# Halves of a batch in turn, joint PE stretches and one written order in a fused attention and two-layer kernel on one core

## The chip, the cores and the metric

The kernel runs on one core of a Trainium2 chip. The metric is the device time in microseconds of one execution; for the kernel before, three runs gave 732.37, 733.7 and 735.04 us, median 733.7 us.

## The reference

For 8 batches of 8 heads, 576 tokens, 64 channels per head and 32 memory slots per head, attention goes through slots. Then a two-layer network runs on all 4608 tokens.

```python
a = softmax(phi, axis=2)                    # per head, over the 576 tokens
k_m, v_m = a^T k, a^T v                     # 32 slots x 64 channels
attn = softmax(q k_m^T / 8, axis=-1)        # over the 32 slots
x = heads of (attn v_m) side by side        # 4608 x 512
h = x @ w_in                                # 512 x 2048
g = where(h > 0, h, exp(min(h, 0)) - 1)     # ELU
out = g @ w_out                             # 2048 x 512
```

## The kernel before

The product of v_m with w_in is taken first (the "w_in product", step `vw`), so that the 2048 hidden channels of a batch come straight from the probabilities: hidden = probabilities times (v_m w_in). All large products run as three passes over a high and a low part of each operand.

**Work items.** A batch has 16 blocks of 128 hidden channels (j) and two halves of 288 tokens (hf). One item is one (batch, half, block); items count from 0 to 255, 32 per batch. An item goes through these steps: `hidden` on PE (L657, six matmuls of 288 columns into one of two PSUM banks named psh), `elu_exp` on ACT (L672, L673), `elu_max` on DVE (L684 for the first 256 tokens, L686 for the other 32, which go to the tile `rest`), `elu_high` on ACT (L698), `elu_low` on DVE (L704), and `project` on PE (L712, six matmuls of 512 columns, into two accumulator banks of the half: pso00 and pso01 for half 0, pso10 and pso11 for half 1). After the last block `collect` copies the accumulators out (ACT and DVE) and `store` writes them. The 32 left-over tokens of each half are gathered for a pair of batches and projected at the pair's end, in eight steps `rest_high`, `rest_low`, `rest_project` that use pso00, then `rest_store`.

**The attention of a batch** is made during the batch before: `load_phi`, `load_e`, `load_kv`, `load_q` on SP's queue; `phi_max` on DVE (L407); `spread_max`, which writes the maxima to DRAM (nmd, L276) and reads them back into all partitions (nmb, L278); `e_shift` on POOL (L289) and `e_exp` on ACT (L294); `slots` (80 small matmuls, L453) and `slots_transpose` (L487) on PE; `scores` for three units of 192 tokens (`by_head`, L502, 64x32 tiles of the array); per unit a softmax on DVE and ACT: `turn`, `softmax_max`, `softmax_shift`, `softmax_exp`, `softmax_sum`, `softmax_divide`, `turn_back`, `probs_high`, `probs_low`. The w_in product is made in four chunks of 512 hidden channels (also `by_head`, L502), each copied out by `vw_high` on ACT (L605) and `vw_low` on DVE (L611). Scores and w_in products share two PSUM banks named psb.

**What sets the order.** Batches 0 and 1, and the attention of batch 2, follow a written list (FIRST) on all engines. After it, each step has a place, a number on the scale of items, and steps are issued in order of places: `hidden` of item i at i - 1.7, `elu_high` at i - 1, `project` at i + 0.6. From there on only PE and SP keep that order; ACT, DVE and POOL take theirs from the framework's scheduler. In batches 2 to 7 the items go block by block with the two halves alternating, so all four accumulators are in use throughout.

```python
    with tc.manual_schedule(engines={mybir.EngineType.PE, mybir.EngineType.SP}):
        with tc.manual_schedule():
            for f, a in first:
                f(*a)
        for _, _, f, a in plan:
            f(*a)
```

Of the kernel before, what the change touches and what calls it, by code (L numbers as in the profile page):

```python
# [16 lines left out]
P = 128  # L17
# [158 lines left out]
def fused_kernel(ctx: ExitStack, tc: tile.TileContext, phiT, phi, kv0, kvt, kv, q0, q1, w_in, w_out, out):  # L176
# [67 lines left out]
    def bank(shape, where):  # L244

        pool, name = {
            "b": (ps_b, "psb"), "h": (ps_h, "psh"),
            "x": (ps_o, "pso01"), "y": (ps_o, "pso10"), "z": (ps_o, "pso11"),
        }[where]
        return pool.tile(shape, F32, name=name)  # L250
# [73 lines left out]

    def load_half_q(b, hf):
        t = work.tile([P, NPAIR, HALF], F32, name="qh", tag="osb", bufs=2 * NB)
# [191 lines left out]

    def turn(b, u):
# [80 lines left out]
    def vw_high(b, c, n0=0, n1=CW):  # L600
        s = st[b]
        if s["vw"][c] is None:
            s["vw"][c] = work.tile([P, 2, 2, CW], F32R, name="vw", tag="vw", bufs=NVB)
        for a, ps in enumerate(s["ps"]["vw", c, n0]):
            nc.scalar.copy(s["vw"][c][:, HI, a, n0:n1], ps)  # L605

    def vw_low(b, c, n0=0, n1=CW):
        s = st[b]
        t = s["vw"][c]
        for a, ps in enumerate(s["ps"].pop(("vw", c, n0))):  # L610
            nc.vector.tensor_tensor(  # L611
                t[:, LO, a, n0:n1], ps, t[:, HI, a, n0:n1], ALU.subtract
            )

# [6 lines left out]
    for b, j0, j1 in blocks:  # L628
# [4 lines left out]
        ]:  # L633
# [42 lines left out]
    def elu_max(it):  # L676
# [7 lines left out]
        nc.vector.scalar_tensor_tensor(gf[:, :n], gf[:, :n], -1.0, ps[:, :n], ALU.add, ALU.max)  # L684
        o = (b % 2 * 2 + hf) * REST
# [43 lines left out]
    def collect(it, t):  # L729
        b, hf, j = order[it]  # L730
        if (b, hf) not in osbs:
            osbs[b, hf] = work.tile([P, NT, DM], F32, name="osb", tag="osb", bufs=2 * NB)
# [52 lines left out]
    def warm_up(n):  # L785
# [8 lines left out]
        for f in (  # L794
# [5 lines left out]
            elu_exp, elu_max, rest_copy, elu_high, elu_low, project, collect, store, rest_high, rest_low,  # L800
# [18 lines left out]
    def softmax(b, u, o, step):  # L819
        at(o, turn, b, u)  # L820
        at(o + step, softmax_max, b, u)
        at(o + 1.01 * step, softmax_shift, b, u)
        at(o + 2 * step, softmax_exp, b, u)
        at(o + 3 * step, softmax_sum, b, u)
        at(o + 3.01 * step, softmax_divide, b, u)
        at(o + 4 * step, turn_back, b, u)
        at(o + 5 * step, probs_high, b, u)
        at(o + 6 * step, probs_low, b, u)

    def products(b, c, o, *cols):  # L830
        at(o, vw, b, c, *cols)
        at(o + (0.3 if cols else 0.75), vw_high, b, c, *cols)
        at(o + (0.31 if cols else 0.76), vw_low, b, c, *cols)

    def attention(b, o):
        at(o - 4, load_phi, b)
# [98 lines left out]
```

## Time and profile before

| what | value |
|---|---|
| median of three runs | 733.7 us (732.37 to 735.04) |
| span of the profiled execution | 730.5 us |
| PE matmul, busy | 706.8 us (97%) |
| PE weight load, busy | 571.2 us (78%) |
| DVE, ACT, POOL, busy | 467.1, 464.9, 44.6 us |
| granted TensorE clock, mean | 0.995 |
| DMA | 64.46 MB, mean 88 GB/s |

The page gives the span, from the first to the last instruction; the profiled execution's own device time is not given apart from it, and the median of the runs lies 3.2 us above the span. A busy share near 100% on PE with the others near 65% says which engine to follow; what share of that busy time is switching or refilling is seen only in the timeline, by the distance from one start to the next.

### The profile page before, as it was taken

What the parts mean: (1) busy time and instruction counts of PE and PEld (TensorE: products, weight loads), DVE (VectorE), ACT (ScalarE), POOL (GpSimd) and SP (SyncE); (2) the same over time, 40 slices, a digit from 0 to 9 for tenths busy, and PEclk for the clock granted to TensorE, in tenths of its full rate; (3) what the DMA queues carried; (4) which work ended last, traced back from release to release, by engine and by line L of the source; (5) the groups of instructions that cost most, each with busy time, mean ns of one, the idle gap of its engine ahead of it and who ended that gap; (6) DMA issues with size and microseconds to landing.
All of it is one profiled execution on the core that took longest, in us unless ns stands there. A gap on an engine that the chain in (4) does not pass through costs nothing.

```text
span 730.5 us, 13669 instructions
## 1 busy us (share of the span) xinstructions
PE 706.8 (97%) x5114; PEld 571.2 (78%) x5114; DVE 467.1 (64%) x1253; ACT 464.9 (64%) x1110; POOL 44.6 (6%) x88
## 2 busy tenths in 40 slices
PE   6698999999999999999999999999999999999997
PEld 5566887887768878877788777887787887888886
DVE  4999898886495467544954449545774547754442
ACT  4779988886456656755655656656565565666552
POOL 0011111122000100010000100000000010000000
PEclk9899999999999999999999999999999999999999
DMA  8961404432316010611015110260002600010002
GB/s 308 369 240 57 175 30 120 146 101 62 102 64 208 27 43 1 247 36 45 2 57 183 56 45 1 76 206 28 19 1 72 223 28 18 1 58 0 2 1 73
DMA packets 24978, 64.46 MB, mean 88 GB/s; under 512 B 3408, under 2 KB 7632, under 8 KB 24912
## 3 DMA queue, kind: packets, MB, share of 16 engines
q1 hardware_dynamic: 24816, 63.46, 25.9%
q8 instruction: 41, 0.67, 0.4%
q14 instruction: 25, 0.20, 0.1%
q10 hardware_dynamic: 96, 0.13, 0.1%
HBM read 54.13 MB, written 9.44 MB: 87 GB/s over the span
## 4 chain that ended last, share of the span: by engine, by line
PE 72%; DMA 12%; DVE 8%; issue 3%; ACT 3%; POOL 1%; SPq 1%; POOLq 0%; DVEq 0%; ACTq 0%
PE pso L712 43%; PE psh L657 22%; DMA nmd<-nm 5%; PE psb L502 4%; DMA nmb<-nmd 3%; DMA ph<-phiT 3%; PE psb L453 2%; POOL e L289 1%; DMA win<-w_in 1%; DMA e<-phi 1%; DVE top L373 1%; DVE gf L681 1%; ACT gf L673 1%; DVE nm L407 1%; DVE vw L611 1%
## 5 line engine op out<-in xcount | busy, mean ns | idle before, releaser
L712 PE MATMUL pso<-wout,gp 128*128 128x512 f32 x1728 | 448.3, 397 | 3.0 <-DVE gp L704 2.3
L712 PEld LDWEIGHTS pso<-wout,gp 128*128 128x128 f32 x1728 | 309.2, 188 | 83.8 <-ACT gf L673 13.0
L657 PEld LDWEIGHTS psh<-A,vw 128*128 128x128 f32 x1536 | 229.2, 188 | 37.5 <-issue 6.2
L657 PE MATMUL psh<-A,vw 128*128 128x288 f32 x1536 | 250.0, 298 | 6.9 <-DVE rest L686 3.4
L684 DVE SCALAR_TENSOR_TENSOR gf<-gf,psh 128x256 f32<-128x256 f32 x192 | 80.5, 419 | 130.1 <-ACT gf L673 129.8
L672 ACT ACTIVATE gf<-psh 128x288 f32<-128x288 f32 x256 | 104.7, 409 | 86.0 <-PE psh L657 84.2
L698 ACT CAST gp<-gf 128x256 fp32r<-128x256 f32 x256 | 103.5, 404 | 87.1 <-DVE gf L684 73.5
L704 DVE TENSOR_TENSOR gp<-gf,gp 128x256 fp32r<-128x256 f32 x256 | 107.6, 421 | 55.2 <-ACT gp L698 54.9
L673 ACT ACTIVATE gf<-gf 128x288 f32<-128x288 f32 x256 | 113.7, 444 | 7.8
L611 DVE TENSOR_TENSOR vw<-psb,vw 128x512 fp32r<-128x512 f32 (+2 forms) x74 | 43.3, 602 | 11.3 <-ACT vw L605 11.1
L289 POOL TENSOR_TENSOR e<-e,nmb 128x512 f32<-128x512 f32 (+1 forms) x18 | 19.7, 1121 | 376.2 <-DMA nmb<-nmd 255.9
L681 DVE SCALAR_TENSOR_TENSOR gf<-gf,psh 128x288 f32<-128x288 f32 x64 | 28.9, 451 | 17.1 <-ACT gf L673 15.9
L605 ACT CAST vw<-psb 128x512 fp32r<-128x512 f32 (+2 forms) x74 | 37.1, 523 | 2.9 <-PE psb L502 0.7
L502 PE MATMUL psb<-win,kvm 64*32 64x512 f32 (+2 forms) x592 | 35.8, 538 | 0.0
L694 POOL COPY rest<-gf 128x32 f32<-128x32 f32 x64 | 24.3, 380 | 165.9 <-DVE gf L681 165.8
L686 DVE SCALAR_TENSOR_TENSOR rest<-gf,psh 128x32 f32<-128x32 f32 x192 | 34.1, 179 | 0.1
L752 ACT CAST gp<-rest 128x256 fp32r<-128x256 f32 x32 | 13.0, 406 | 23.8 <-PE pso L712 21.8
L373 DVE SCALAR_TENSOR_TENSOR top<-mag,top 128x512 uint32<-128x512 uint32 x32 | 22.2, 693 | 1.9 <-ACT mag L364 0.3
L757 DVE TENSOR_TENSOR gp<-rest,gp 128x256 fp32r<-128x256 f32 x32 | 13.4, 418 | 15.0 <-ACT gp L752 14.9
L368 ACT ACTIVATE mag<-raw 128x512 uint32<-128x512 uint32 x30 | 20.1, 672 | 2.5 <-DVE top L373 2.5
L294 ACT ACTIVATE e<-e 128x512 f32<-128x512 f32 (+1 forms) x18 | 9.8, 559 | 16.4 <-POOL e L289 16.3
L364 ACT ACTIVATE mag<-raw 128x512 f32<-128x512 f32 x30 | 19.5, 666 | 0.4 <-DVE win L385 0.4
(96 smaller groups left out, 369.2 us busy)
## 6 DMA issues: line engine op xcount, KB each, us to landing
kvt<-kv SPq DMA_DIRECT2D x32, 512.0 KB, 7.3
out<-osb SPq DMA_DIRECT2D x16, 512.0 KB, 2.8
raw<-w_in SPq DMA_DIRECT2D x15, 512.0 KB, 7.1
raw<-w_out SPq DMA_DIRECT2D x15, 512.0 KB, 8.1
qt<-q SPq DMA_DIRECT2D x18, 384.0 KB, 4.2
ph<-phiT SPq DMA_DIRECT2D x7, 576.0 KB, 4.8
e<-phi SPq DMA_DIRECT2D x12, 256.0 KB, 6.4
qh<-q SPq DMA_DIRECT2D x4, 576.0 KB, 11.5
```

The costliest lines, as they stand in the source:

```text
L502: nc.tensor.matmul(outs[a][32 * j : 32 * j + 32, :], lhs[r, 32 * j : 32 * j + 32], rhs[r, j], start=True, stop=True, tile_position=(64 * a ...
L605: nc.scalar.copy(s["vw"][c][:, HI, a, n0:n1], ps)
L611: nc.vector.tensor_tensor(t[:, LO, a, n0:n1], ps, t[:, HI, a, n0:n1], ALU.subtract)
L657: nc.tensor.matmul(ps, t[:, x, g, c0 : c0 + P], s["A"][hf][:, y, g, :], start=(n == 0), stop=(n == 5),)
L672: nc.scalar.activation(gf, ps, AF.Relu, scale=-1.0)
L673: nc.scalar.activation(gf, gf, AF.Exp, scale=-1.0)
L681: nc.vector.scalar_tensor_tensor(gf, gf, -1.0, ps, ALU.add, ALU.max)
L684: nc.vector.scalar_tensor_tensor(gf[:, :n], gf[:, :n], -1.0, ps[:, :n], ALU.add, ALU.max)
L686: nc.vector.scalar_tensor_tensor(rest_of(b, j)[:, o : o + REST], gf[:, n:], -1.0, ps[:, n:], ALU.add, ALU.max)
L698: nc.scalar.copy(gp[:, HI], gs[it][:, : NT * P])
L704: eng.tensor_tensor(gp[:, LO], gf[:, : NT * P], gp[:, HI], ALU.subtract)
L712: nc.tensor.matmul(ps, gp[:, y], wout[j][:, x, :], start=(first and n == 0), stop=(last and n == 2),)
```

## The change

In batches 2 to 7 the items now go through all 16 blocks of half 0 and then of half 1. The accumulators of the half that is not running are idle, and `scores_of` and `products` borrow them: the three units of scores become one stretch on PE (place base - 14.6, base being the batch's first item), and the four w_in chunks become two stretches of two (base - 7.1 and base + 2.9). Since every chunk is needed by both halves, all four are kept: the fourth takes a buffer ("c3") that holds the queries and the output of batch 1 earlier. `elu_rest` is split from `elu_max`, and is placed later for the first two items of batches 4 and 6, while the rests of the pair before are still read. All steps of the attention have new places, counted from o = base - 32, and after FIRST all engines follow places; FIRST itself is the same text.

```diff
@@ -245,7 +245,8 @@
         pool, name = {
             "b": (ps_b, "psb"), "h": (ps_h, "psh"),
-            "x": (ps_o, "pso01"), "y": (ps_o, "pso10"), "z": (ps_o, "pso11"),
+            "w": (ps_o, "pso00"), "x": (ps_o, "pso01"),
+            "y": (ps_o, "pso10"), "z": (ps_o, "pso11"),
         }[where]
         return pool.tile(shape, F32, name=name)
@@ -322,8 +323,19 @@
         nc.sync.dma_start(t, q1[b - NB, :, u])
         st[b]["q"][u] = t
+    late_c = {}
+    def half_of_1(hf):
+        if "t" not in late_c:
+            late_c["t"] = work.tile([P, 2, NPAIR * HALF], F32, name="one", tag="c3", bufs=1)
+        return late_c["t"][:, hf]
     def load_half_q(b, hf):
-        t = work.tile([P, NPAIR, HALF], F32, name="qh", tag="osb", bufs=2 * NB)
+        if b == 0:
+            t = work.tile([P, NPAIR, HALF], F32, name="qh", tag="osb", bufs=2)
+        else:
+            t = half_of_1(hf).rearrange("p (a n) -> p a n", a=NPAIR)
         t0 = hf * HALF
         nc.sync.dma_start(t, q0[b, :, hf])
         for u, (u0, u1) in enumerate(units(b)):
@@ -516,6 +528,16 @@
         by_head(ps, s["kvm"][:, 0], q)
         s["ps"]["s", u] = ps
+    def scores_of(b, own, lent):
+        s = st[b]
+        first = [bank([P, 2, UT], x) for x in own]
+        last = [bank([P, UT], x) for x in lent]
+        for u in range(NU):
+            ps = [x[:, u] for x in first] if u < 2 else last
+            by_head(ps, s["kvm"][:, 0], s["q"][u])
+            s["ps"]["s", u] = ps
     def turn(b, u):
         s = st[b]
@@ -597,28 +619,21 @@
         by_head(ps, s["kvm"][:, 1], win[c][:, :, n0:n1])
         s["ps"]["vw", c, n0] = ps
-    def vw_high(b, c, n0=0, n1=CW):
+    def vw_high(b, c, n0=0, n1=CW, parts=(0, 1)):
         s = st[b]
         if s["vw"][c] is None:
-            s["vw"][c] = work.tile([P, 2, 2, CW], F32R, name="vw", tag="vw", bufs=NVB)
-        for a, ps in enumerate(s["ps"]["vw", c, n0]):
-            nc.scalar.copy(s["vw"][c][:, HI, a, n0:n1], ps)
-    def vw_low(b, c, n0=0, n1=CW):
+            home = dict(tag="c3", bufs=1) if b >= NB and c == NVC - 1 else dict(tag="vw", bufs=NVB)
+            s["vw"][c] = work.tile([P, 2, 2, CW], F32R, name="vw", **home)
+        for a in parts:
+            nc.scalar.copy(s["vw"][c][:, HI, a, n0:n1], s["ps"]["vw", c, n0][a])
+    def vw_low(b, c, n0=0, n1=CW, parts=(0, 1)):
         s = st[b]
         t = s["vw"][c]
-        for a, ps in enumerate(s["ps"].pop(("vw", c, n0))):
+        for a in parts:
             nc.vector.tensor_tensor(
-                t[:, LO, a, n0:n1], ps, t[:, HI, a, n0:n1], ALU.subtract
+                t[:, LO, a, n0:n1], s["ps"]["vw", c, n0][a], t[:, HI, a, n0:n1], ALU.subtract
             )
     blocks = [(0, 0, 4), (1, 0, 4), (0, 4, 8), (1, 4, 12), (0, 8, 16), (1, 12, 16)]
     blocks += [(b, 0, NJ) for b in range(NB, B)]
@@ -630,7 +645,7 @@
         seen.add(b)
         for hf, j in turns if len(order) == 0 else [
             (hf, j) for j in range(j0, j1) for hf in range(2)
-        ]:
+        ] if b < NB else [(hf, j) for hf in range(2) for j in range(NJ)]:
             order.append((b, hf, j))
             ends.append((new, j == j0, j == j1 - 1))
@@ -682,6 +697,12 @@
             return
         n = NT * P
         nc.vector.scalar_tensor_tensor(gf[:, :n], gf[:, :n], -1.0, ps[:, :n], ALU.add, ALU.max)
+        gs["ps", it] = gf, ps
+    def elu_rest(it):
+        b, hf, j = order[it]
+        gf, ps = gs.pop(("ps", it))
+        n = NT * P
         o = (b % 2 * 2 + hf) * REST
         nc.vector.scalar_tensor_tensor(
             rest_of(b, j)[:, o : o + REST], gf[:, n:], -1.0, ps[:, n:], ALU.add, ALU.max
@@ -729,7 +750,11 @@
     def collect(it, t):
         b, hf, j = order[it]
         if (b, hf) not in osbs:
-            osbs[b, hf] = work.tile([P, NT, DM], F32, name="osb", tag="osb", bufs=2 * NB)
+            if b == 1:
+                o = half_of_1(hf)[:, : NT * DM].rearrange("p (t n) -> p t n", t=NT)
+            else:
+                o = work.tile([P, NT, DM], F32, name="osb", tag="osb", bufs=2)
+            osbs[b, hf] = o
         osb = osbs[b, hf][:, t, :]
         ps = acc[b, hf][t]
         if not ends[it][0]:
...
@@ -816,59 +841,71 @@
         if (f, a) not in done:
             plan.append((place, len(plan), f, a))
-    def softmax(b, u, o, step):
-        at(o, turn, b, u)
-        at(o + step, softmax_max, b, u)
-        at(o + 1.01 * step, softmax_shift, b, u)
-        at(o + 2 * step, softmax_exp, b, u)
-        at(o + 3 * step, softmax_sum, b, u)
-        at(o + 3.01 * step, softmax_divide, b, u)
-        at(o + 4 * step, turn_back, b, u)
-        at(o + 5 * step, probs_high, b, u)
-        at(o + 6 * step, probs_low, b, u)
-    def products(b, c, o, *cols):
-        at(o, vw, b, c, *cols)
-        at(o + (0.3 if cols else 0.75), vw_high, b, c, *cols)
-        at(o + (0.31 if cols else 0.76), vw_low, b, c, *cols)
+    def softmax(b, u, o, *steps):
+        turned, shifted, exped, divided, back, parts = (o + x for x in steps)
+        at(turned, turn, b, u)
+        at(shifted, softmax_max, b, u)
+        at(shifted + 0.01, softmax_shift, b, u)
+        at(exped, softmax_exp, b, u)
+        at(divided, softmax_sum, b, u)
+        at(divided + 0.01, softmax_divide, b, u)
+        at(back, turn_back, b, u)
+        at(parts, probs_high, b, u)
+        at(parts + 0.01, probs_low, b, u)
+    def products(b, o, c, lent, *copies):
+        for i, own in enumerate(("bb", lent)):
+            at(o, vw, b, c + i, 0, CW, own)
+        for n, x in enumerate(copies):
+            at(o + x, vw_high, b, c + n // 2, 0, CW, (n % 2,))
+            at(o + x + 0.01, vw_low, b, c + n // 2, 0, CW, (n % 2,))
     def attention(b, o):
-        at(o - 4, load_phi, b)
+        at(o + 0.5, load_phi, b)
+        for u in range(3):
+            at(o + 1 + 0.1 * u, load_e, b, u)
+        at(o + 3.5, phi_max, b)
+        at(o + 3.6, spread_max, b)
         for c in range(NCH):
-            at(o - 3 + c, load_kv, b, c)
+            at(o + 3.7 + 0.01 * c, load_kv, b, c)
+        at(o + 3.8, load_q, b, 0)
+        for g in range(2):
+            at(o + 5.5 + g, phi_exp, b, g)
+        at(o + 7.5, slot_scale, b)
         for u in range(3):
-            at(o + 4 + u, load_q, b, u)
-            at(o - 3 + u, load_e, b, u)
-            at(o + 1.1 + u, e_shift, b, u)
-            at(o + 2.1 + u, e_exp, b, u)
-        at(o + 0.1, phi_max, b)
-        for g in range(2):
-            at(o + 0.12, phi_exp, b, g)
-        at(o + 1.1, slot_scale, b)
-        at(o + 1, spread_max, b)
+            at(o + 8, e_shift, b, u)
+            at(o + 9.5 + u, e_exp, b, u)
         for c in range(NCH):
-            at(o + 5.4, slots, b, c)
-        at(o + 6.1, slots_copy, b)
-        at(o + 7.2, slots_transpose, b)
-        at(o + 7.4, kv_copy, b)
+            at(o + 12.4, slots, b, c)
+        at(o + 12.5, load_q, b, 1)
+        at(o + 12.6, load_q, b, 2)
+        at(o + 13.5, slots_copy, b)
+        at(o + 14.4, slots_transpose, b)
+        at(o + 14.5, kv_copy, b)
+        at(o + 17.4, scores_of, b, "bb", "wx")
         for u in range(3):
-            i = o + 8.2 + 2 * u
-            at(i, scores, b, u)
-            softmax(b, u, i + 0.7, 0.3)
+            softmax(b, u, o + 18.5 + 2.5 * u, 0, 1, 2, 3, 4, 5)
+    softmax(NB, 2, 54, 0, 0, 0, 0, 0, 0)
     for b in range(2, B):
         base = 2 * NJ * b
-        attention(b, 43 if b == 2 else base - 22)
-        for c in range(NVC):
-            products(b, c, base - 7.6 + 8 * c)
+        if b > NB:
+            attention(b, base - 32)
+            products(b, base - 7.1, 0, "wx", 0.6, 1.6, 2.6, 3.6)
+        products(b, base + 2.9, 2, "yz", 0.6, 1.6, 2.6, 3.6)
     for it, (b, hf, j) in enumerate(order):
         at(it - 1.7, hidden, it)
         at(it - 1.69, elu_exp, it)
         at(it - 1.68, elu_max, it)
         if b < NB:
             at(it - 1.67, rest_copy, it)
-        at(it - 1, elu_high, it)
-        at(it - 0.99, elu_low, it)
+        elif b > NB and b % 2 == 0 and order[max(it - 2, 0)][0] != b:
+            at(32 * b - 0.34 + 0.005 * (it - 32 * b), elu_rest, it)
+        else:
+            at(it - 1.67, elu_rest, it)
+        late = 0.695 if it and b != order[it - 1][0] and b % 2 == 0 and b > NB else 0
+        at(it - 1 + late, elu_high, it)
+        at(it - 0.99 + late, elu_low, it)
         at(it + 0.6, project, it)
         if ends[it][2]:
             for t in range(NT):
@@ -883,10 +920,9 @@
                     at(it + 0.81, rest_store, b // 2)
     plan.sort(key=lambda x: x[:2])
-    with tc.manual_schedule(engines={mybir.EngineType.PE, mybir.EngineType.SP}):
-        with tc.manual_schedule():
-            for f, a in first:
-                f(*a)
+    with tc.manual_schedule():
+        for f, a in first:
+            f(*a)
         for _, _, f, a in plan:
             f(*a)
```

**PE, scores of batch 5 (while batch 4 runs).** L502 (L514 in the changed kernel) is `by_head`, L657 (L672) `hidden`, L712 (L733) `project`. Of before, two of the three stretches:

```order
L502 MATMUL psb<-qt,kvm 32x192 x8
L657 MATMUL psh<-A,vw 128x288 x6
L712 MATMUL pso_4739<-wout_1635,gp 128x512 x3
L712 MATMUL pso_4740<-wout_1635,gp 128x512 x3
L657 MATMUL psh<-A,vw 128x288 x6
L712 MATMUL pso_4767<-wout_1635,gp 128x512 x3
L712 MATMUL pso_4768<-wout_1635,gp 128x512 x3
L502 MATMUL psb<-qt,kvm 32x192 x8
```

Of the change:

```order
L672 MATMUL psh<-A,vw 128x288 x6
L514 MATMUL psb<-qt,kvm 32x192 x16
L514 MATMUL pso_5222<-qt,kvm 32x192 x4
L514 MATMUL pso_5223<-qt,kvm 32x192 x4
L733 MATMUL pso_5197<-wout_485,gp 128x512 x3
L733 MATMUL pso_5198<-wout_485,gp 128x512 x3
L672 MATMUL psh<-A,vw 128x288 x6
L733 MATMUL pso_5197<-wout_572,gp 128x512 x3
L733 MATMUL pso_5198<-wout_572,gp 128x512 x3
```

The three stretches of one unit, with items between them, became one stretch of three units; the last unit goes to the two accumulators of half 0.

**ACT, e_exp of batch 5.** L294 (L295) is `e_exp`, L672, L673 (L687, L688) `elu_exp`, L698 (L719) `elu_high`, L605 `vw_high`. Of before:

```order
L672 ACTIVATE gf<-psh 128x288
L673 ACTIVATE gf<-gf 128x288
L294 ACTIVATE e<-e 128x512
L605 CAST vw<-psb 128x512
L698 CAST gp<-gf 128x256
L605 CAST vw<-psb 128x512
L294 ACTIVATE e<-e 128x512
L294 ACTIVATE e<-e 64x256
L672 ACTIVATE gf<-psh 128x288
```

Of the change:

```order
L687 ACTIVATE gf<-psh 128x288
L688 ACTIVATE gf<-gf 128x288
L295 ACTIVATE e<-e 128x512
L719 CAST gp<-gf 128x256
L687 ACTIVATE gf<-psh 128x288
L688 ACTIVATE gf<-gf 128x288
L295 ACTIVATE e<-e 128x512
L719 CAST gp<-gf 128x256
L687 ACTIVATE gf<-psh 128x288
L688 ACTIVATE gf<-gf 128x288
L295 ACTIVATE e<-e 64x256
L719 CAST gp<-gf 128x256
```

Each of the three now stands between the `elu_exp` and the `elu_high` of a different item, and the copies of a w_in chunk are no longer among them.

**SP, loads of batch 4's attention.** ph is phi for the maxima, e is phi for the slots, kvt is k and v, nmd and nmb are the maxima on their way through DRAM. Of before:

```order
L260 DMA ph<-phiT 128x1152
L300 DMA kvt<-kv 128x1024
L267 DMA e<-phi 128x2x256
L300 DMA kvt<-kv 128x1024
L267 DMA e<-phi 128x2x256
L300 DMA kvt<-kv 128x1024
L267 DMA e<-phi 64x256
L300 DMA kvt<-kv 128x1024
L300 DMA kvt<-kv 64x1024
L276 DMA nmd<-nm 128x2
L278 DMA nmb<-nmd 128x256
```

Of the change:

```order
L261 DMA ph<-phiT 128x1152
L268 DMA e<-phi 128x2x256 x2
L268 DMA e<-phi 64x256
L277 DMA nmd<-nm 128x2
L279 DMA nmb<-nmd 128x256
L301 DMA kvt<-kv 128x1024 x4
L301 DMA kvt<-kv 64x1024
```

The two transfers of the maxima moved ahead of the five k and v loads.

## Rows read from the trace of the kernel before

**Rows 1.** The page, busy times: engine, busy us (share of the span), instructions.
```profile
PE 706.8 (97%) x5114; PEld 571.2 (78%) x5114; DVE 467.1 (64%) x1253; ACT 464.9 (64%) x1110; POOL 44.6 (6%) x88
```

**Rows 2.** Timeline of PE in batch 5: start us, us, engine, line, operation, count.
```profile
470.21 0.96 PE L657 MATMUL psh<-A,vw 128*128 128x288 f32 x6
471.10 1.09 PE L502 MATMUL psb<-win,kvm 64*32 64x512 f32 x16
472.12 1.66 PE L712 MATMUL pso<-wout,gp 128*128 128x512 f32 x6
473.62 0.96 PE L657 MATMUL psh<-A,vw 128*128 128x288 f32 x6
474.41 1.56 PE L712 MATMUL pso<-wout,gp 128*128 128x512 f32 x6
475.81 0.96 PE L657 MATMUL psh<-A,vw 128*128 128x288 f32 x6
```

**Rows 3.** Timeline of PE in batch 4, around one scores stretch.
```profile
439.94 1.55 PE L712 MATMUL pso<-wout,gp 128*128 128x512 f32 x6
441.42 0.56 PE L502 MATMUL psb<-qt,kvm 64*32 64x192 f32 x16
441.91 1.07 PE L657 MATMUL psh<-A,vw 128*128 128x288 f32 x6
442.82 1.53 PE L712 MATMUL pso<-wout,gp 128*128 128x512 f32 x6
```

**Rows 4.** Timeline of PE in batches 0 and 1: a lone stretch, then adjoining ones.
```profile
40.61 0.45 PE L502 MATMUL pso<-win,kvm 64*32 64x128 f32 x16
40.99 1.66 PE L712 MATMUL pso<-wout,gp 128*128 128x512 f32 x6
...
46.49 0.45 PE L502 MATMUL psb<-win,kvm 64*32 64x128 f32 x16
46.73 0.48 PE L502 MATMUL pso<-qh,kvm 64*32 64x160 f32 x16
```

**Rows 5.** Waits of PE over the whole span: us in total, times, longest us.
```profile
PE psh L657 <- DVE rest L686: 3.4, 5, 1.2
```

**Rows 6.** Timeline of PE in batch 5, around the longest of these waits.
```profile
493.14 1.56 PE L712 MATMUL pso<-wout,gp 128*128 128x512 f32 x6
495.87 1.03 PE L657 MATMUL psh<-A,vw 128*128 128x288 f32 x6 [1.17 <-DVE rest L686]
496.74 1.54 PE L712 MATMUL pso<-wout,gp 128*128 128x512 f32 x6
```

**Rows 7.** Chain that ended last, in order of time: start us, us, what.
```profile
167.60 2.94 DMA nmd<-nm
...
398.17 7.31 DMA nmd<-nm
405.53 5.53 DMA nmb<-nmd
```

**Rows 8.** Timeline of all engines in batch 4, where the wait of ACT begins.
```profile
411.22 3.28 POOL L289 TENSOR_TENSOR e<-e,nmb 128x512 f32<-128x512 f32 x3 [89.62 <-DMA nmb<-nmd]
...
412.56 0.63 ACT L294 ACTIVATE e<-e 128x512 f32<-128x512 f32 x1 [2.60 <-POOL e L289]
```

**Rows 9.** Windows: us, busy (instructions) by engine, PE clock, DMA share, GB/s.
```profile
164.00:168.00 4.00, 4.00 (x30) 2.35 (x30) 3.57 (x7) 3.18 (x8) 1.15 (x2) 1.00 0.00 0
398.00:402.00 4.00, 4.00 (x23) 3.42 (x23) 2.27 (x10) 3.60 (x11) 0.00 (x0) 1.00 1.04 371
440.00:460.00 20.00, 20.00 (x145) 15.75 (x144) 17.78 (x54) 13.27 (x32) 0.00 (x0) 1.00 0.00 1
```

**Rows 10.** Timeline near the end: last step of one ELU, and its project.
```profile
708.57 0.43 DVE L704 TENSOR_TENSOR gp<-gf,gp 128x256 fp32r<-128x256 f32 x1 [0.38 <-ACT gp L698]
...
710.95 1.33 PE L712 MATMUL pso<-wout,gp 128*128 128x512 f32 x5
```

**Rows 11.** Timeline of SP's DMA queue: the three q loads of batch 3.
```profile
234.93 20.39 SPq L322 DMA_DIRECT2D qt<-q  x3
```

More of the change, by code (lines that the diff above doesn't have):

```diff
@@ L799, in fused_kernel @@
             softmax_divide, turn_back, probs_high, probs_low, vw, vw_high, vw_low, hidden,
-            elu_exp, elu_max, rest_copy, elu_high, elu_low, project, collect, store, rest_high, rest_low,
+            elu_exp, elu_max, elu_rest, rest_copy, elu_high, elu_low, project, collect, store, rest_high, rest_low,
             rest_project, rest_store,
```

## Prediction

> **What bounds the kernel now.** I read the page first: PE is busy 97% of the span [rows 1], so only what PE executes, or waits for, can move the time. A busy share cannot tell products from refilling, so I read PE's timeline next, by the distance from one start to the next. [...] Two things break this beat. One is a stretch of small 64x32 matmuls (w_in products, scores). The other is the list of PE's waits: after the start it holds one large entry, `hidden` waiting five times, 3.4 us together, until DVE's `rest` frees a psh bank [rows 5].
>
> **Term A: stretches joined on PE.** A lone w_in chunk costs more than itself: `hidden` to stretch 0.89 instead of 0.79, the stretch 1.02 to the next start, then 1.50 instead of 1.40, so 0.10 + 1.02 + 0.10 = 1.22 us [rows 2]. A lone unit of scores costs (1.48 - 1.40) + 0.49 + (0.91 - 0.79) = 0.69 us [rows 3]. Before, batches 3 to 7 have three scores stretches and four chunks each; batch 2's last two chunks come in the changed part as well. After, the order printed above shows one stretch of scores, and w_in chunks in pairs.
>
> The part that surely goes is entering and leaving. Scores: 3 x 0.69 = 2.07 becomes 0.08 + 3 x 0.49 + 0.12 = 1.67, a saving of 0.40. A pair of chunks, which now stands between `project` and `hidden` like a scores stretch: 2 x 1.22 = 2.44 becomes 0.08 + 2 x 1.02 + 0.12 = 2.24, a saving of 0.20. Per batch 0.40 + 2 x 0.20 = 0.80; five batches and batch 2's pair: 4.2 us. This is the lower end.
>
> Inside a joint stretch more may go. A lone stretch of 128 columns takes 0.38 us to the next start (40.61 to 40.99), one that runs straight on into another small product 0.24 (46.49 to 46.73) [rows 4]: 0.14 less. Per batch four such inner borders (two of scores, one in each pair) and one in batch 2, 21 in all: 21 x 0.14 = 2.9 us. I take it, since rows 4 are the same kind of product in the same tile shape: A = 4.2 + 2.9 = **7.1 us**, ends 4.2 and 7.1.
>
> [...] The rows show 0.20 at entering and leaving and 0.14 inside, so I stay with them.
>
> **Term B: the five waits.** In the longest one, `project` to `hidden` takes 2.73 instead of 1.40, and the next distance is 0.87 instead of 0.79: 1.41 us lost where the row says 1.17 of idle time [rows 6], so some 0.24 of refilling each time. Five times: 3.4 + 5 x 0.24 = **4.6 us**, ends 3.4 and 4.6. What is late there: ACT has sat 2.60 us at `e_exp`, which waits for POOL's `e_shift`, which waits for nmb [rows 8]; behind `e_exp` in ACT's queue stand the w_in copies and the `elu_exp` that PE's bank hangs on. And nmb is late since nmd takes 7.31 and nmb 5.53 us [rows 7]: they were issued behind the k and v loads, with the DMA engines full (share 1.04, 371 GB/s). In batch 2 nmd was issued with idle engines (share 0.00) and took 2.94 us [rows 7, 9].
>
> After the change `phi_max` stands at place o + 3.5 and `e_exp` at o + 9.5, 9.5 and more, six items, 13.1 us. Ahead of nmd only phi and e are issued, loads that SP starts about three items earlier; the k and v loads come behind nmb. The chain is then some 2.9 + 5.5 us and 1.34 us of `e_shift` (411.22 to 412.56) [rows 8], 9.8 us: 3 us to spare. So the wait goes. Late next are the k and v loads themselves: issued about 3 us after nmd, needed by `slots` at o + 12.4, nine items or 19.5 us after `phi_max`. They are hidden.
>
> **Term C: order of DVE and ACT.** Both now run strictly in places. The crowded part is o + 21 to o + 29, where softmax steps and four w_in copies fall together: counted from the places, 24 ELU instructions of 8 items and 31 others on DVE, 55 in 8 x 2.19 + 2 = 19.5 us. Before, a stretch of 20.0 us held 54 such instructions, busy 17.78, and PE did not wait (20.00 busy) [rows 9]. At 17.78/54 = 0.33 each the 55 need 18.1 us. Should the 2.2 us in which DVE sat idle there be needed too, it is 20.3, or 0.8 over. Against that stands the slack of an item: `elu_low` ended at 709.00, its `project` began at 710.95 [rows 10], 1.95 us. Ends: nothing lost, or 5 x 0.8 = 4.0. I take 0.1 per batch, **0.5 us** lost, close to the row without a wait.
>
> **Edits at no cost.** Half after half: each item keeps its six and six matmuls; `collect` of half 0 moves to the middle of a batch, where PE uses other banks. `elu_rest`: the same instruction, later for four items; at the start of batches 4 and 6 PE has 48 matmuls of the rests to run, which cover it; if not, PE waits for a psh bank as in term B. The buffer "c3": its copy in batch 2 waits for batch 1's store, issued at place 63.8 and needed at 69.5, 12 us later. At the end the copies of the last half stand behind the eight rest steps, but these finish three `rest_project` steps before PE does. Batches 0 and 1: the same order on every engine.
>
> **Sum.** 7.1 + 4.6 - 0.5 = 11.2 us, all in the profiled execution. Its span is 3.2 us under the median; the part outside is not touched, so I take it from the median: 733.7 - 11.2 = **722.5 us**.
>
> **Rivals.**
> 1. *Only entering and leaving is saved* (inside a joint stretch each product drains as if alone): 722.5 + 2.9 = 725.4. For it: I have only one border row of 0.24. Against it: that row. Chance 0.15.
> 2. *The waits come back in another place*: nmd stays slow, or the crowded part stalls PE. Then B is not won: 722.5 + 4.6 = 727.1. For it: ACT now cannot take a later `elu_exp` ahead of a waiting `e_exp`. Against it: 3 us to spare. Chance 0.14.
> 3. *POOL holds DVE up.* Before, DVE had little to do during `e_shift`, since ACT stood still; after, `elu_low` runs beside it. If the three `e_shift` (3.28 us) [rows 8] held DVE throughout, 3.28 - 1.95 = 1.33 us of PE would be lost five times: 722.5 + 6.7 = 729.2. Nothing in the rows has both engines at work long enough to tell. Chance 0.06. [...]
> 4. *Slower: the joint scores wait for their last query tile.* Before, unit 0 needed only its own load; now PE's whole queue stands behind three, two of which SP issues only when `slots` has freed their buffers. From `slots` to the joint scores PE has five items, 11 us. In batch 3 SP needed 20.39 us to issue three such loads, because it waited for buffers [rows 11]. If the last tile landed 20.4 us after `slots`, PE would stand 9.4 us five times: 722.5 + 47 = 769. Slower than before by more than 2.2 us it is from (11.2 + 2.2)/5 = 2.7 us of standing per batch, that is a landing 13.7 us after `slots`. Against it: SP has nothing in front of these loads but `slots`. Chance 0.04.
>
> That the change does not do what it says is ruled out for the stretches by the printed order.
>
> **Chances and range.** Forecast 0.61, rivals 0.15, 0.14, 0.06, 0.04. A measurement of this kernel tells about 0.3%, 2.2 us, from no change. Forecast and rivals 1 and 2 are faster by more; rival 3 half so, if rival 1 or 2 comes along within 0.3%: faster 0.93, same 0.03, slower 0.04. The range starts at 719.5: no loss in C, and the 1.3 us by which the three runs differ from their median, and a little more refilling than 0.24 in the short waits. It ends at 728.5, beyond rivals 1 and 2 with 1.4 us for the runs.
>
> **What would show it.** PE's timeline: in batches 3 to 7 one scores stretch and two w_in pairs, a pair some 1.9 us from its start to the next `hidden`, and scores some 1.2. PE's wait for `rest` gone from the list, nmd near 3 us, ACT without the 2.6 us at `e_exp`. Wrong: a pair at 2.04 or more (rival 1); a new line for `hidden` or `project` in PE's waits (2, 3); a PE wait at the scores for a q load (4).

## The result, and the profile after

| | before | after |
|---|---|---|
| median of the runs | 734.28 us (732.37 to 735.04, 4 runs) | 723.12 us (722.7 to 724.27, 4 runs) |
| span of the profiled execution | 730.5 us | 720.9 us |
| PE matmul, busy | 706.8 us | 700.8 us |

The ratio is 0.9864, 95% interval 0.9839 to 0.989: 11.2 us less, where 11.2 was predicted (723.1 us, where 722.5 was). The profiled spans differ by only 9.6 us, because the first part, whose written order is the same, took 1.3 us longer in the profiled run of after. From `hidden` of item 64 to PE's last product the trace of before has 511.59 us and that of after 500.74, which is 10.85 less; the terms below are counted there, in what is called the changed part from here on.

The page of after, its line on PE [rows 1]:

```profile
PE 700.8 (97%) x5114; PEld 575.8 (80%) x5114; DVE 465.0 (64%) x1253; ACT 460.7 (64%) x1110; POOL 45.6 (6%) x88
```

The share is 97% as before, so the page alone would not show that anything changed. PE's timeline does [rows 2, 3]; the columns are start, length, engine, line, operation and count. First the pair of batch 2, then the scores of batch 3:

```profile
225.11 1.55 PE L733 MATMUL pso<-wout,gp 128*128 128x512 f32 x6
226.59 1.09 PE L514 MATMUL psb<-win,kvm 64*32 64x512 f32 x16
227.48 1.06 PE L514 MATMUL pso<-win,kvm 64*32 64x512 f32 x16
228.47 1.07 PE L672 MATMUL psh<-A,vw 128*128 128x288 f32 x6
229.38 1.55 PE L733 MATMUL pso<-wout,gp 128*128 128x512 f32 x6
...
262.07 0.95 PE L672 MATMUL psh<-A,vw 128*128 128x288 f32 x6
262.95 0.88 PE L514 MATMUL psb<-qt,kvm 64*32 64x192 f32 x32
263.62 0.53 PE L514 MATMUL pso<-qt,kvm 64*32 64x192 f32 x16
264.08 1.66 PE L733 MATMUL pso<-wout,gp 128*128 128x512 f32 x6
265.58 0.96 PE L672 MATMUL psh<-A,vw 128*128 128x288 f32 x6
```

Read by starts: the pair takes 228.47 - 226.59 = 1.88 us, plus 0.09 at entering (1.48 against 1.39, the median of after) and 0.11 at leaving (0.91 against 0.80). That is about 2.08 us for two chunks that cost 1.22 each before. The scores take 264.08 - 262.95 = 1.13, plus 0.09 and 0.10, so 1.32 us for what was 3 x 0.69 = 2.07. All 11 pairs and 5 scores stretches read the same within 0.03.

The five waits for `rest` [rows 5] are gone from PE's list. Two losses of the changed part are new, in the timeline:

```profile
220.61 0.73 PE L733 MATMUL pso<-wout,gp 128*128 128x512 f32 x2 [0.65 <-ACT orest L796]
...
375.38 12.98 PE L733 MATMUL pso<-wout,gp 128*128 128x512 f32 x54
...
376.82 0.19 PEld L733 LDWEIGHTS pso<-wout,gp 128*128 128x128 f32 x1 [0.31 <-ACT gp L777]
```

Both are the price of a strict order on ACT: `rest_store` and the first `rest_high` stand behind an `elu_exp` for which nothing is in a hurry. The first costs 0.8 us once; the second makes the boundary of a pair of batches, from the start of the 54 matmuls to the next `hidden`, 12.82 us (375.38 to 388.20) instead of 12.36 (377.00 to 389.36 in the trace of before), and 12.78 instead of 12.37 the second time.

The chain from the maxima to `e_exp` [rows 7, 8], for the last attention (batch 7), first in the timeline of before:

```profile
569.63 1.10 SPq L300 DMA_DIRECT2D kvt<-kv  x2
570.06 1.35 DVE L407 TENSOR_REDUCE nm<-ph 128x2 f32<-128x1152 f32 x1 [0.81 <-DMA ph<-phiT]
571.44 0.34 SPq L276 DMA_DIRECT2D nmd<-nm  x1
...
579.31 0.33 SPq L278 DMA_DIRECT2D nmb<-nmd  x1
584.02 3.28 POOL L289 TENSOR_TENSOR e<-e,nmb 128x512 f32<-128x512 f32 x3 [89.14 <-DMA nmb<-nmd]
585.36 0.63 ACT L294 ACTIVATE e<-e 128x512 f32<-128x512 f32 x1 [2.14 <-POOL e L289]
```

And in the timeline of after:

```profile
567.70 1.35 DVE L419 TENSOR_REDUCE nm<-ph 128x2 f32<-128x1152 f32 x1
569.08 0.35 SPq L277 DMA_DIRECT2D nmd<-nm  x1
...
572.43 0.34 SPq L279 DMA_DIRECT2D nmb<-nmd  x1
...
572.86 3.79 SPq L301 DMA_DIRECT2D kvt<-kv  x5
...
577.97 3.46 POOL L290 TENSOR_TENSOR e<-e,nmb 128x512 f32<-128x512 f32 x3 [86.81 <-DMA nmb<-nmd]
580.26 0.61 ACT L295 ACTIVATE e<-e 128x512 f32<-128x512 f32 x1
```

Two lengths are to be read from such rows. The **chain** runs from the end of the reduction to the first shifted tile: before 571.41 to 585.35 (POOL's start and 1.33 for one of its three), 13.9 us; after 569.05 to 579.30, 10.2 us. The **distance** runs from the same end to the moment at which ACT has come to `e_exp`: before 585.36 - 2.14 = 583.22, so 11.8 us; after 580.26, so 11.2 us. ACT waits for the difference, if the chain is the longer one. The shorter chain is the gain; the distance even fell a little.

### The profile page after: what moved, and what is told of

It is laid out like the page before. It is cut to its first block, busy times and chain, and to the rows that moved or that the text cites. A ratio compares the mean times of both kernels' runs of the same rounds, so it can differ in the third digit from the quotient of the medians.

```text
span 720.9 us, 13704 instructions
## 1 busy us (share of the span) xinstructions
PE 700.8 (97%) x5114; PEld 575.8 (80%) x5114; DVE 465.0 (64%) x1253; ACT 460.7 (64%) x1110; POOL 45.6 (6%) x88
## 4 chain that ended last, share of the span: by engine, by line
PE 87%; DVE 8%; DMA 2%; ACT 1%; issue 1%; SPq 0%; POOL 0%; DVEq 0%; POOLq 0%; ACTq 0%
PE pso L733 53%; PE psh L672 27%; PE psb L514 3%; PE psb L465 2%; PE pso L514 2%; DMA kvt<-kvt 1%; DMA e<-phi 1%; DVE gf L696 1%; DVE top L385 1%; DVE sm L572 1%; DVE vw L634 0%; DVE top L397 0%; DMA nmd<-nm 0%; DVE gp L725 0%; DVE mx L554 0%
## 5 line engine op out<-in xcount | busy, mean ns | idle before, releaser
L733 PE MATMUL pso<-wout,gp 128*128 128x512 f32 x1728 | 448.4, 397 | 3.7 <-DVE gp L725 2.3
L733 PEld LDWEIGHTS pso<-wout,gp 128*128 128x128 f32 x1728 | 309.0, 188 | 69.6 <-DVE gp L725 4.2
L672 PEld LDWEIGHTS psh<-A,vw 128*128 128x128 f32 x1536 | 230.9, 189 | 36.8 <-issue 10.2
L672 PE MATMUL psh<-A,vw 128*128 128x288 f32 x1536 | 248.7, 297 | 3.6 <-DVE spare L547 1.9
L687 ACT ACTIVATE gf<-psh 128x288 f32<-128x288 f32 x256 | 104.8, 409 | 106.6 <-PE psh L672 104.8
L719 ACT CAST gp<-gf 128x256 fp32r<-128x256 f32 x256 | 103.5, 405 | 81.2 <-DVE gf L699 65.9
L725 DVE TENSOR_TENSOR gp<-gf,gp 128x256 fp32r<-128x256 f32 x256 | 109.1, 427 | 50.2 <-ACT gp L719 49.5
L688 ACT ACTIVATE gf<-gf 128x288 f32<-128x288 f32 x256 | 113.9, 445 | 8.1
L634 DVE TENSOR_TENSOR vw<-psb,vw 128x512 fp32r<-128x512 f32 (+2 forms) x52 | 28.4, 569 | 1.9 <-ACT vw L628 1.8
L628 ACT CAST vw<-psb 128x512 fp32r<-128x512 f32 (+2 forms) x52 | 23.7, 486 | 0.7 <-PE psb L514 0.7
L514 PE MATMUL psb<-win,kvm 64*32 64x512 f32 (+2 forms) x416 | 23.8, 511 | 0.3 <-DVE win L397 0.3
L782 DVE TENSOR_TENSOR gp<-rest,gp 128x256 fp32r<-128x256 f32 x32 | 13.1, 419 | 16.2 <-ACT gp L777 16.1
L634 DVE TENSOR_TENSOR vw<-pso,vw 128x512 fp32r<-128x512 f32 (+1 forms) x26 | 16.0, 620 | 0.0
```

The source lines that it names most:

```text
L514: nc.tensor.matmul(outs[a][32 * j : 32 * j + 32, :], lhs[r, 32 * j : 32 * j + 32], rhs[r, j], start=True, stop=True, tile_position=(64 * a ...
L634: nc.vector.tensor_tensor(t[:, LO, a, n0:n1], s["ps"]["vw", c, n0][a], t[:, HI, a, n0:n1], ALU.subtract)
L672: nc.tensor.matmul(ps, t[:, x, g, c0 : c0 + P], s["A"][hf][:, y, g, :], start=(n == 0), stop=(n == 5),)
L687: nc.scalar.activation(gf, ps, AF.Relu, scale=-1.0)
L688: nc.scalar.activation(gf, gf, AF.Exp, scale=-1.0)
L719: nc.scalar.copy(gp[:, HI], gs[it][:, : NT * P])
```

## The experiments

Unless said otherwise an edit is made to the changed kernel; places are those of its table. Ratios are against the kernel before, which ran beside each. Medians of different rounds scatter by 1 us and more, so the length of the changed part in the trace stands beside them (511.6 us before, 500.7 after); it leaves out the first part, which took 214.5 to 217.9 us in these traces though no edit changes its written order.

**The two joint stretches, each undone alone.** The three scores units one by one again:

```diff
-        at(o + 17.4, scores_of, b, "bb", "wx")
         for u in range(3):
+            at(o + 17.4 + 2.5 * u, scores, b, u)
```

> The changed kernel with the three units of scores in three stretches again, two and a half items apart, in the psb banks; everything else stays. Theory (each border between the small 64x32 products and the full ones costs PE about 0.34 us): in batches 3 to 7 three stretches of 0.69 us in place of one of 1.32 us, 0.75 us more per batch, 3.7 us in all: some 727 us, PE without new waits. Rival (the joint stretches save little, and the gain is the order of the other engines): within 1 us of the changed kernel's 723.1 us.

Measured: 726.31 us (725.2 to 726.75), ratio 0.9906 (0.9884 to 0.9929), 3.2 us more than after; the changed part takes 503.7 us, 3.0 more. That is 0.7 less than expected: one of the three units now stands just ahead of the `project` that was late in after anyway (term C below), so its leaving adds nothing there, some 0.5 us over the five batches. In its timeline a unit stands alone again, and pays at both borders (0.89 to enter, 0.48, and 1.50 for the next `project`):

```profile
263.07 0.95 PE L672 MATMUL psh<-A,vw 128*128 128x288 f32 x6
263.96 0.56 PE L514 MATMUL psb<-qt,kvm 64*32 64x192 f32 x16
264.44 1.66 PE L733 MATMUL pso<-wout,gp 128*128 128x512 f32 x6
265.94 0.96 PE L672 MATMUL psh<-A,vw 128*128 128x288 f32 x6
```

And the two chunks of a pair one item apart (`at(o, vw, ...)` to `at(o + i, vw, ...)` in `products`):

> The changed kernel with each pair of w_in chunks made in two stretches, one item apart, in the same banks and with the same copies; everything else stays. Theory (borders): two stretches of 1.22 us in place of one pair of 2.08 us, 0.36 us more per pair, eleven pairs: 4.0 us, some 727 us. Rival (inside a pair each product drains as if alone, so only entering and leaving counts, 0.2 us per pair): 2.2 us more, 725.3 us; rival (no effect): 723.1 us.

Measured: 727.13 us (726.92 to 728.59), ratio 0.9924 (0.9901 to 0.9947), 4.0 us more, and the changed part takes 504.7 us, 4.0 more as well. The two together give 7.2 us by the medians and 7.0 by the traces: term A is shown by taking each half of it away.

**The order of SP's queue, undone alone.** The k and v loads go ahead of the two transfers of the maxima again, as before the change:

```diff
-            at(o + 3.7 + 0.01 * c, load_kv, b, c)
+            at(o + 1.3 + 0.01 * c, load_kv, b, c)
```

> The changed kernel with one edit on SP: the five k and v loads are issued before the two transfers of the maxima, as in the kernel before. Theory (the waits of PE came from the maxima queued behind k and v): nmd takes 7 to 8 us again instead of 2.9, e_exp comes up before e_shift is done, ACT sits some 2.6 us, PE waits for a psh bank in all five attentions, about 1 us each: 5 us more, some 728 us. Rival (the waits went because e_exp no longer stands among the w_in copies and one at a time): nmd is slow but PE does not wait, 723 us.

Measured: 722.39 us (721.23 to 723.46), ratio 0.986 (0.9834 to 0.9886): nothing lost, and the changed part takes 500.8 us. The loads stand ahead of the transfers as they did before, yet the chain is short. Its timeline says why:

```profile
561.04 2.98 SPq L301 DMA_DIRECT2D kvt<-kv  x5
566.23 1.35 DVE L419 TENSOR_REDUCE nm<-ph 128x2 f32<-128x1152 f32 x1
567.60 0.33 SPq L277 DMA_DIRECT2D nmd<-nm  x1
...
572.32 0.33 SPq L279 DMA_DIRECT2D nmb<-nmd  x1
...
576.66 3.48 POOL L290 TENSOR_TENSOR e<-e,nmb 128x512 f32<-128x512 f32 x3 [87.57 <-DMA nmb<-nmd]
578.79 0.61 ACT L295 ACTIVATE e<-e 128x512 f32<-128x512 f32 x1
```

The last k and v load has been issued at 564.02 and nmd follows 3.6 us later: nmd takes 4.7 us, nmb 4.3, the chain 10.4. In the kernel before the last one had been issued at 570.73, 0.7 us ahead of nmd, and nmd took 7.9. There nmd landed just behind the last of these loads, at 579.25 behind 579.10, and in the first whole window of 4 us behind its issue (572 to 576) the DMA share was 1.07; here the share was down to 0.45 in the window behind the issue of nmd (568 to 572). So in these two kernels it is the time between the loads and the small transfer that counts, and not their order alone. Since nmd was not slow again, this run does not show what a long chain would cost in the written order, and it leaves its own rival open, that the waits went because `e_exp` no longer stands among the w_in copies.

**The scheduler back on ACT, DVE and POOL.** After FIRST only PE and SP keep places, as before the change:

> The changed kernel with ACT, DVE and POOL left to the framework's scheduler after the written list, PE and SP in places as before; it puts e_exp one or two items after phi_exp, where the places put it three or more. Theory (what matters is the distance from phi_max to e_exp against the 9.8 us of the transfers and e_shift): ACT waits 1 to 4 us at e_exp and PE loses up to 2 us in each of five attentions: 723 to 733 us, with e_shift or psh in PE's waits. Rival (the joint stretches are the whole gain and the order is worth nothing): within 1 us of 723.1 us and no PE wait.

Measured: 757.14 us (755.93 to 759.09), ratio 1.0332 (1.0304 to 1.0359), slower than either kernel by far and 24 us over the end of the expected range; the changed part takes 535.1 us, 34.4 more than after. PE's waits, then ACT's (us in total, times, longest):

```profile
PE pso L733 <- ACT gp L719: 19.0, 4, 5.1
PE psh L672 <- DVE rest L707: 5.9, 1, 5.9
```

```profile
ACT e L295 <- POOL e L290: 30.2, 11, 5.4
```

The chain is as short as in after (10.2 us in the last attention), but the scheduler puts `e_exp` one or two `elu_exp` behind `phi_exp`: the distance there is 5.1 us. PE stood 24.9 us in five waits where up to 2 us each were expected, and around each of them its granted clock fell (0.83 to 0.93 in the windows of 20 us), which the expectation did not have. This led to the theory that the difference of chain and distance decides, and to three runs on it.

**The distance alone.** First `e_exp` three items nearer, and `e_shift`, alone on POOL, ahead of it:

```diff
-            at(o + 8, e_shift, b, u)
-            at(o + 9.5 + u, e_exp, b, u)
+            at(o + 5, e_shift, b, u)
+            at(o + 6.5 + u, e_exp, b, u)
```

> The changed kernel with e_exp three items nearer to phi_max (places o + 6.5, 7.5 and 8.5 in place of o + 9.5, 10.5 and 11.5) and e_shift issued on POOL ahead of it; nothing else moves, and the k and v loads still stand behind the two transfers of the maxima. Theory (the distance from phi_max to e_exp decides): the chain after phi_max is 2.9 + 5.4 + 1.3 = 9.6 us, the distance now 3 items or 6.6 us, so ACT sits about 3.0 us at e_exp in each of batches 3 to 7. By the kernel before, where a wait of 2.60 on ACT cost PE 1.41 us, PE loses some 1.8 us five times: 732, between 730 and 735, and the wait of hidden or project for the ELU is back in PE's list with five entries. Rival (what matters is that nothing stands ahead of the transfers on SP): no wait, 723.

Then one and a half items nearer (o + 8 + u):

> As the run before it, but e_exp only one and a half items nearer (places o + 8, 9 and 10). Theory: distance 4.5 items or 9.9 us against a chain of 9.6, so ACT hardly waits: 723 to 724, no new entry in PE's waits. If instead the chain or the distance is read wrongly by more than about 1 us, ACT waits up to 2 us and the time is 726 or more. Rival (order on SP): 723.

Measured: three items 745.28 us (744.76 to 747.15), ratio 1.0161 (1.0128 to 1.0195); one and a half 728.56 us (727.91 to 730.38), ratio 0.9936 (0.9913 to 0.9959). The changed part takes 522.9 and 506.1 us, 22.1 and 5.3 more than after. PE's waits for the ELU, first with three items, then with one and a half:

```profile
PE pso L733 <- ACT gp L719: 13.6, 5, 3.2
```

```profile
PE pso L733 <- ACT gp L719: 2.8, 4, 0.8
```

Direction and mechanism are as the theory says, both losses larger than it said. One part of the miss is the conversion of places into time: I had counted items from the place of `phi_max`, 6.6 and 9.9 us, while the distances measured from the end of the reduction are 6.1 and 7.2 us; the chain, 9.6 us by the theory, is 8.8 to 10.4. The price on PE was too low as well: the 1.41 us that the theory sets beside a wait of 2.60 us on ACT stands in the trace of before beside one of 3.41 (`e_exp` at 492.94). With one and a half items PE stands 2.8 us, and the other 2.5 us or so (5.3 less 2.8) are time lost beyond the idle time, which the prediction calls refilling, at a granted clock of 1.00 in every window from 220 us to 700. The `e_exp` of this run stand apart from the w_in copies and PE loses about as much as before the change, which speaks against the rival that the run with k and v first left open. With three items there is the clock besides. In that run PE's granted clock fell in the attention of batch 3 (windows of 1 us: PE's busy time, granted clock, DMA share, GB/s; then the timeline):

```profile
241.00:242.00 1.00, 0.00 (x0) 1.00 1.04 426
...
243.00:244.00 1.00, 0.75 (x2) 0.50 1.05 430
...
248.00:249.00 1.00, 1.00 (x4) 0.50 0.55 194
249.00:250.00 1.00, 1.00 (x6) 0.76 0.01 3
```

```profile
239.46 0.96 PE L672 MATMUL psh<-A,vw 128*128 128x288 f32 x6
243.25 3.07 PE L733 MATMUL pso<-wout,gp 128*128 128x512 f32 x6 [2.83 <-ACT gp L719]
246.12 1.64 PE L672 MATMUL psh<-A,vw 128*128 128x288 f32 x6
247.56 2.43 PE L733 MATMUL pso<-wout,gp 128*128 128x512 f32 x6
249.82 0.95 PE L672 MATMUL psh<-A,vw 128*128 128x288 f32 x6
```

PE had stood for 2.83 us; its granted clock was then 0.50 until about 249.5 (0.76 in the window from 249 to 250, 1.00 in the next). From 239.46 to 249.82 two items took 10.36 us instead of 4.38. Here the standing and refilling cost 3.0 us, and the lower clock, with what refilling lies in these distances, another 3.0 (1.47 + 0.65 + 0.86 over three). In windows of 20 us the granted clock was below 1.00 in three of the five attentions of this run (0.83, 0.91, 0.91), and in none of the run with one and a half items, where PE stood for less than 1 us at a time.

**The new order of loads without the written order.** The kernel before, with the k and v loads at o + 1.01 (its own places), behind the maxima:

> The kernel before, with one thing of the change: the k and v loads of batches 3 to 7 are issued behind the two transfers of the maxima. The order that the scheduler then finds on ACT has e_exp two or three elu_exp behind phi_exp, where the kernel before had five or six. Prediction as it stood (the transfers are late because k and v were issued ahead of them): nmd falls to about 3 us, the five waits go, 4.9 us less than before: 729. Theory after the runs so far (distance decides, and a scheduler spends what a shorter transfer gives): nmd falls to about 3 us, but e_exp stands nearer, ACT waits 3 to 5.5 us at it, and PE loses more than before: 736 to 748.

Measured: 757.32 us (754.14 to 760.02), ratio 1.0323 (1.0271 to 1.0375): 24 us slower, 9 us over the theory's range. The changed part takes 534.5 us, 22.9 more than before. The chain in the last attention is 10.2 us, but the distance 5.3; PE stands 18.0 us in six waits of up to 3.9 us (3.4 us in five before), and in four of the five attentions its granted clock fell (0.83 to 0.94 in windows of 20 us).

Read as above, in the last attention of each kernel:

| kernel, last attention | chain | distance | ACT waits | time |
|---|---|---|---|---|
| before | 13.9 us | 11.8 us | 2.14 us | 734.3 us |
| after | 10.2 | 11.2 | 0 | 723.1 |
| k and v first | 10.4 | 11.2 | 0 | 722.4 |
| `e_exp` 1.5 items nearer | 10.2 | 7.2 | 2.97 | 728.6 |
| `e_exp` 3 items nearer | 10.1 | 6.1 | 4.01 | 745.3 |
| scheduler on ACT, DVE, POOL | 10.2 | 5.1 | 5.09 | 757.1 |
| before, k and v behind | 10.2 | 5.3 | 4.83 | 757.3 |

In each row the wait is the chain less the distance, or nothing where the distance is the longer. The way in which the two are read makes it so; what the runs add is that moving `e_exp` nearer (with `e_shift` ahead of it on POOL), with a chain about as long as in after, brought the wait and the loss. Two things were not run: a long chain in the written order (13.9 us against 11.2 would make ACT wait 2.7 us by the same arithmetic), and a longer distance in the kernel before with nothing else changed.

**The small losses.** `rest_high` and `rest_low` of a pair's first step ahead of the boundary's second `elu_exp`, and `rest_store` of batch 1 ahead of `elu_exp` of item 65:

```diff
-                        at(it + 0.61 + 0.01 * i, rest_high, b // 2, i)
-                        at(it + 0.611 + 0.01 * i, rest_low, b // 2, i)
+                        h = it + (0.305 if i == 0 else 0.61 + 0.01 * i)
+                        at(h, rest_high, b // 2, i)
+                        at(h + 0.001, rest_low, b // 2, i)
...
-                    at(it + 0.81, rest_store, b // 2)
+                    at(it + (0.81 if b > 1 else 0.2), rest_store, b // 2)
```

> The changed kernel with the first rest copies of batches 3 and 5 (rest_high, rest_low) ahead of the second elu_exp of the boundary, and the rest store of batch 1 ahead of elu_exp(65) on ACT. Theory: the two losses that the changed kernel shows beside the forecast's terms go: 0.45 us at each of two boundaries with a following 0.1, and 0.8 us at the start of batch 2, so 1.9 us less than the changed kernel's 723.1: 721.2, and PE's wait of project for ACT's orest (0.65 us) is gone. Rival (these are waits which PE would meet an item later anyway): 723.1, and the wait shows up in the next row.

Measured: 721.11 us (719.5 to 722.13), ratio 0.9835 (0.9812 to 0.9857); the changed part takes 499.2 us, 1.5 less than after. PE's entry for orest is gone, and the boundaries take 12.42 and 12.37 us instead of 12.82 and 12.78. Its median is below those of both kernels, though the interval of its ratio overlaps that of after.

Then term C. With the softmax steps (0, 1.55, 2.3, 3.3, 4.3, 5) for the third unit:

> The run before it, and in each of batches 3 to 7 the max and shift of the third softmax unit half an item later, behind elu_low of the crowded item. Theory: the project just before each joint w_in pair takes 1.40 us instead of 1.50, five times, so 0.5 us less than the run before it: 720.7. Rival (DVE is simply full there, and the steps collide with the next item's elu_max): no change, 721.2 or more, with the 0.1 in another project.

Measured: 722.0 us (720.76 to 722.4), ratio 0.9845 (0.9825 to 0.9866), no gain (changed part 499.5 us). I had moved the wrong unit: the max and shift that stand ahead of `elu_low` in after are those of the second. Moved there, with steps (0, 1.05, 2, 3, 4, 5) for it:

> The run with the earlier rests, and in each of batches 3 to 7 the max and shift of the second softmax unit (not of the third, as in the run before) behind elu_low of the item whose project stands before the joint w_in pair. The run that moved the third unit left the order there as it was, and the project kept its 1.50 us. Theory (term C: these two DVE steps, 1.05 us, make elu_low late): that project takes 1.40 in place of 1.50, five times, so 0.5 us less than with the earlier rests alone: 720.6, and PE's entry of a weight load waiting for elu_low falls by five times 0.17. Rival (DVE is full there, the next elu_max or transpose is late instead): no change, 721.1, with the 0.1 in another row of the beat.

Measured: 720.89 us (720.11 to 723.1), ratio 0.9852 (0.9831 to 0.9873). The timeline of after at the place in batch 3, and that of this run:

```profile
276.02 0.55 DVE L554 TENSOR_REDUCE mx<-sc 128x12 f32<-128x384 f32 x1
...
276.60 0.56 DVE L562 TENSOR_TENSOR sc<-sc,mx 128x384 f32<-128x384 f32 x1
277.07 0.42 DVE L725 TENSOR_TENSOR gp<-gf,gp 128x256 fp32r<-128x256 f32 x1
...
277.31 1.67 PE L733 MATMUL pso<-wout,gp 128*128 128x512 f32 x6
```

```profile
274.75 0.42 DVE L725 TENSOR_TENSOR gp<-gf,gp 128x256 fp32r<-128x256 f32 x1
...
275.08 0.55 DVE L554 TENSOR_REDUCE mx<-sc 128x12 f32<-128x384 f32 x1
...
276.04 1.55 PE L733 MATMUL pso<-wout,gp 128*128 128x512 f32 x6
```

In after `elu_low` starts 0.24 us ahead of its `project`, here 1.29 us, and all five such distances fall from 1.50 or 1.51 to 1.40. The changed part takes 498.5 us, 0.7 less than with the earlier rests alone. So the traces show the 0.5 us; the times can't, since 0.2 us between the medians is within the scatter.

## Why the prediction was right, step by step

**Term A, 7.1 us: right in kind, 7.45 in size.** Summed over all rows the small stretches and their borders cost 36.96 us before and 29.51 after. The forecast pair had 0.20 at its borders and 0.14 less inside, 2.10 us; it measured 2.08. The scores were put at 1.39 and measured 1.32: their inner borders save a little more than 0.14. Rival 1 (nothing saved inside, a pair at 2.24) is out. Entering and leaving cost 0.09 to 0.11 each.

**Term B, 4.6 us: right in size (4.9), its working only in part.** The five waits cost 1.08, 0.72, 0.89, 1.34 and 0.43 us in `project` to `hidden` and some 0.08 each after; all are gone. That nmd was late behind the loads is borne out for the kernel before (nmb is issued 7.87 us behind nmd in its last attention, 3.35 in that of after). In the working two attentions are mixed: the loss of 1.41 us on PE [rows 6] goes with a wait of 3.41 us on ACT, and the wait of 2.60 [rows 8] with a loss of 0.96. And the step "3 us to spare" was wrong: it set 13.1 us between two places against a chain that starts only when the reduction ends. Measured from there to `e_exp` it is 11.2 us, the chain 10.2, and over the five attentions ACT came 0.9 to 1.5 us after the tile was ready. That 1 us was enough where 3 were counted on is in part luck: 4 us less of distance cost 5.3 us. Nor was the order of the loads on SP what this needed: with the loads 3.6 us ahead of nmd nothing is lost. Taken alone the new order even costs 24 us, since the scheduler then places `e_exp` nearer. What carries term B, as far as these runs show, is that the written order keeps the distance while the chain gets shorter.

**Term C, 0.5 us lost: right (0.55),** and at the place named: DVE's crowded part, 0.11 in the last `project` before the pair in each of five batches. The 2.19 us per item in its sum is the distance from one `hidden` to the next, 473.62 to 475.81 [rows 2]. The run with the second unit's steps moved takes it away again.

**Edits at no cost: two of them cost 1.9 us.** I wrote that the 48 matmuls of the rests cover the boundary of a pair. They cover the late `elu_rest`, but not the first `rest_high`, without which those matmuls can't start: 2 x (0.45 + 0.10). And `rest_store` of batch 1 behind an `elu_exp` was not seen: 0.8. Against that the `slots_transpose` stretches, which now stand between `hidden` and `project`, give back about 0.14 five times (0.37 to 0.23 over their three distances), which was not in the sum either. So 7.45 + 4.9 - 0.55 - 1.9 + 0.7 = 10.6 of the 10.85 us; 0.25 is assigned to no row. That the sum comes out within 0.4 us of the 11.2 forecast is in part luck: the 1.9 us that were not foreseen are offset by 0.35 and 0.3 more in terms A and B, the 0.7, and the 0.25.

**The rivals.** Nothing waits for a query tile (rival 4). Rival 2's mechanism is real, as the runs with a shorter distance show; here some 1 us of slack keeps it away. Rival 3's is real as well (`elu_low` 1.24 and 1.37 us beside a shift, 0.42 without; last section), and covered.

## What to carry to other kernels

A step that waits for a transfer, on an engine with a fixed order, is judged by two lengths read from the same starting event: how long the chain to its data takes, and how far behind that event the engine reaches it; shortening the first helps only if the second stays. Small products of another tile shape are worth grouping: here each stretch saved pays about 0.2 us at its borders and 0.14 to 0.16 inside. When engines change from a scheduler to a written order, look at the first step of every boundary for instructions that now stand behind work which is in no hurry.

## What the runs showed of the hardware that was not expected

`elu_low` on DVE beside `e_shift` on POOL, in the timeline of after:

```profile
319.13 3.47 POOL L290 TENSOR_TENSOR e<-e,nmb 128x512 f32<-128x512 f32 x3 [74.39 <-DMA nmb<-nmd]
...
320.75 1.24 DVE L725 TENSOR_TENSOR gp<-gf,gp 128x256 fp32r<-128x256 f32 x1 [0.38 <-ACT gp L719]
322.93 0.42 DVE L725 TENSOR_TENSOR gp<-gf,gp 128x256 fp32r<-128x256 f32 x1 [0.37 <-ACT gp L719]
```

The same DVE instruction takes 1.24 us beside POOL's shift and 0.42 behind it, and POOL's three shifts 3.47 us instead of 3.28. Once more, at 489.17, `elu_low` took 1.37 us. At 410.73 it was the other way round: `elu_low` kept its 0.43 us, and the POOL shift that started 0.02 us behind it took 1.58 us instead of 1.31. `elu_max`, which reads one of its inputs from PSUM, took 0.41 or 0.42 us in all ten cases in which it ran beside a shift. `project` did not wait (PE busy 7.00 us of the 7 from 318 to 325), because it needs this tile only an item later.

The other surprise is how much a stand of PE of about 3 us can cost beyond itself: in the attention of batch 3 above the granted clock of 0.50 took the loss from 3.0 to 6.0 us, and in that of batch 7 of the same run, after 2.92 us of standing, the clock stayed at 1.00. In the three runs that lost 22 us and more PE stood fifteen times for 1.8 to 5.9 us in the changed part, and twelve times the granted clock in the windows of 20 us around it fell below 1.00 (0.83 to 0.94). The shortest stand with a fall is 2.83 us, the longest without one 2.92, so the length alone does not tell them apart; why one and not the other stays open.
